# A mixer and an MLP under one gate on one core: reordered opening, half-built tables, u added straight from PSUM, state rotations on GpSimd

## The chip, the cores and the metric

One core of a Trainium2 chip runs the kernel in one launch. The metric is device time in microseconds, lower is better.

## What is computed

Input x has 2048 tokens of 1024 features. One branch is a diagonal complex state-space layer, the other a layer norm and an MLP of 3584 hidden units; a sigmoid of x·gate_w mixes them for each token:

```
Lam_bar = exp(exp(log_dt) * (Lambda_re + 1j*Lambda_im))
Bu      = x @ (((Lam_bar - 1)/Lam)[:, None] * (B_re + 1j*B_im)).T
h[t]    = Lam_bar * h[t-1] + Bu[t]                 # 2048 steps, 1024 states
a = 2*real(h @ C.T) + x*Dskip
b = gelu(layernorm(x) @ w1 + b1) @ w2 + b2
out = g*a + (1-g)*b,   g = sigmoid(sum(x*gate_w))
```

## The kernel before, in words

Every piece of work is a task with an engine, a duration that its author wrote down, a priority and its buffers. `Graph.schedule` plays the tasks through a list scheduler, and each engine's instructions are emitted in the order found. So the priorities and durations in the code set the order, and each engine then runs its own list strictly in order.

TensorE's (PE's) program has four parts: the products u = x·B, the MLP (blocks m and b), and the output products y. Nearly all products are 2x2 block products done with seven block multiplications (Strassen-Winograd, class `SG`, steps `p1` to `p7`), whose operand sums VectorE (DVE) makes beforehand (`b_sums`, `x_sums`, `x_sum4`, line 1119). A step of an u group is four matmuls of 512 columns. Steps p7 and p4 of a group use the same PSUM bank one after the other, with two other steps between them.

The opening makes the transposed operands. PE transposes the first four 128-token pieces of x (`t_x`, line 801) and the first B blocks (`t_b0`, line 874; `t_b`, line 825, for blocks 1 to 3); DVE and ScalarE (ACT) copy them out. The other three quarters of x (`xT_dma`, line 1232, called xT1 to xT3) and B blocks 4 to 7 (`bT_dma`, line 1316) are transposed by the DMA. All these loads stand in the queue of SyncE (SP). Nine matmuls on zeros (`em_warm`, line 845) run ahead of the first transpose.

Then come the plain products of block 0 (`bu_plain`, lines 1147 and 1032), the groups (1,0), (2,0), (3,0) on the first half of the tokens, and the other groups. The gate logits (`z_gate`, line 1289) are 32 narrow matmuls over all four quarters of x; they stand in the second group, (2,0).

`bu_group.fin` takes u out of PSUM. Of its two results that need an addition, the real one is added by DVE straight from PSUM (line 1218); the imaginary one is copied by ACT to a buffer `uc` (line 1221) and added by DVE from there (line 1223).

The scan of the states runs on DVE in 16 units (`ssm`, two halves of the states by eight pieces of 256 tokens) spread over the MLP. Each unit rotates u with tables of cosines and sines (line 1412 and 1415), scans (line 1426), and rotates back; the state that goes on to the next unit is rotated by three small operations on 8 numbers per partition (`fx1` to `fx3`, lines 1435, 1437, 1439). The tables are built by doubling in eight rounds of six DVE operations (line 972).

Of the kernel before, what the change touches and what calls it, by code (L numbers as in the profile page):

```python
# [171 lines left out]
class Graph:  # L172
# [43 lines left out]
    def dma(self, prio, emit, nbytes, sem, reads=(), writes=(), name="", xpose=False, extra=(), ndma=1, bw=None, thr=False, q="sp"):  # L216
# [3 lines left out]
        if xpose:  # L220
            idur = max(idur, XPOSE_ISSUE_PER_MB * nbytes / 1e6)
# [3 lines left out]
    def _schedule_once(self):  # L225
# [27 lines left out]
        while ev:  # L253
# [17 lines left out]
            for e in engs:  # L271
# [25 lines left out]
                if t.kind == "dma":  # L297
                    issue_end = st + t.dur
                    push(issue_end, 1, e)
                    ts = max(issue_end, chan_free[e])  # L300
                    busy_o = sum(1 for o in chan_free if o != e and chan_free[o] > ts)
                    bw_eff = t.bw * (1.0, 0.55, 0.4)[busy_o]
                    chan_free[e] = ts + t.nbytes / bw_eff
                    t.finish = chan_free[e] + DMA_LAT
# [76 lines left out]
    def _schedule_latest(self, ls):  # L381
# [57 lines left out]
        while ev:  # L439
# [8 lines left out]
            for e in engs:  # L448
# [13 lines left out]
                if t.kind == "dma":  # L462
                    issued = t.start + t.dur
                    push(issued, 1, e)
                    ts = max(issued, chan_free[e])
                    others = sum(1 for o in chan_free if o != e and chan_free[o] > ts)
                    chan_free[e] = ts + t.nbytes / (t.bw * (1.0, 0.55, 0.4)[others])
                    t.finish = chan_free[e] + DMA_LAT
# [97 lines left out]
def build(nc, A_x, A_Lambda_re, A_Lambda_im, A_B_re, A_B_im, A_C_re, A_C_im, A_log_dt, A_Dskip,  # L566
# [25 lines left out]
    with es:  # L592
# [81 lines left out]
        tfirst = [7, 3, 6, 0, 1, 2, 5]  # L674
# [57 lines left out]
        g.dma(P0, emit_cst_loads, NROW * 256, sem("d_cst"), writes=[b_stg], name="cst_loads", ndma=len(vecs), q="act")  # L732
# [43 lines left out]
        def load_b(pt, prio):  # L776
# [9 lines left out]
            g.dma(prio, em, 2 * 128 * D * 2, ssem("bnat", s), writes=[v], name="bnat%d" % pt, ndma=2)  # L786
# [4 lines left out]
        def t_x(k, prio):  # L791
# [11 lines left out]
            o_chain(g.add("pe", 0.06 * DT, prio, em, reads=[v, b_ident], writes=[b_ps[bk], b_ps[bk2]], name="xT_T%d" % k, extra=list(o_last)))  # L803
# [63 lines left out]
        def t_b0(ri, prio):  # L867
# [9 lines left out]
            if ri == 0:  # L877
                o_chain(t)
# [1068 lines left out]
```

## Time and profile before

| | before |
|---|---|
| median of 3 runs | 551.43 us (551.0 to 551.49) |
| profiled execution, its own time | 554.73 us |
| its span | 553.0 us |
| busy: PE, DVE, ACT, GpSimd (POOL) | 546.1, 510.2, 287.1, 89.7 us |

The span runs from the first to the last instruction of the profiled execution; 1.73 us of its own time lie outside. "PEld" is PE's weight load, "PEclk" the granted TensorE clock (1.00 is 2.4 GHz, 0.50 is 1.2 GHz), "SPq" and "POOLq" are issues of DMAs.

### The profile page before, as it was taken

How to read it: one execution, taken by the hardware profiler on the slowest of the kernel's cores; microseconds unless marked ns; L12 is line 12 of the kernel's file. 1: busy time of each engine (PE TensorE's matmuls, PEld its weight loads, DVE VectorE, ACT ScalarE, POOL GpSimd, SP SyncE). 2: the span in 40 equal slices, each digit the busy share in tenths (PEclk: the TensorE clock that was granted, in tenths of full speed). 3: DMA queues.
4: the chain of work that ended last, by engine and by line, in shares of the span. 5: the costliest groups of instructions: out<-in, count | busy, mean ns of one | idle time of the engine just before them, and what ended most of it. 6: DMA issues, size and time to landing. Idle time of an engine off the chain costs nothing.

```text
span 553.0 us, 7464 instructions
## 1 busy us (share of the span) xinstructions
PE 546.1 (99%) x2622; PEld 250.2 (45%) x2622; DVE 510.2 (92%) x880; ACT 287.1 (52%) x480; POOL 89.7 (16%) x146
## 2 busy tenths in 40 slices
PE   8899999999999999999999999999999999999997
PEld 5444444444444444444444444444444444444443
DVE  5879989999999999999999999999999999899863
ACT  3767887886773347773347762247672322111110
POOL 0127662540001010001110000220000111001000
PEclk9989999999999999999999999999999999999999
DMA  9996999789762455464666983797767999987531
GB/s 268 252 301 155 272 272 293 252 274 360 237 142 105 164 190 206 148 216 196 225 227 184 310 167 64 135 200 226 240 157 136 230 312 298 376 293 249 180 117 57
DMA packets 115054, 120.07 MB, mean 217 GB/s; under 512 B 70338, under 2 KB 92738, under 8 KB 113994
## 3 DMA queue, kind: packets, MB, share of 16 engines
q1 hardware_dynamic: 102400, 73.69, 47.9%
q0 software_dynamic: 12480, 45.90, 26.8%
q8 instruction: 20, 0.33, 0.2%
q14 instruction: 16, 0.13, 0.1%
q10 hardware_dynamic: 138, 0.02, 0.0%
HBM read 56.40 MB, written 47.46 MB: 188 GB/s over the span
## 4 chain that ended last, share of the span: by engine, by line
PE 94%; SPq 3%; DMA 2%; issue 0%; DVE 0%
PE ps L1034 71%; PE ps L1032 22%; SPq L1232 2%; DMA ar<-in_A_x_dram 2%; PE ps L1289 1%; PE ps L1100 0%; SPq L771 0%; SPq L784 0%; SPq L783 0%; SPq L857 0%; DVE ar L1732 0%
## 5 line engine op out<-in xcount | busy, mean ns | idle before, releaser
L1034 PE MATMUL ps<-ar 128*128 128x512 f16 (+1 forms) x1844 | 416.9, 379 | 0.0
L1034 PEld LDWEIGHTS ps<-ar 128*128 128x128 f16 (+1 forms) x1844 | 180.1, 98 | 218.1 <-issue 1.3
L1032 PE MATMUL ps<-ar 128*128 128x512 bf16 (+1 forms) x608 | 150.0, 379 | 0.0
L1119 DVE TENSOR_TENSOR ar<-ar 128x512 f16<-128x512 bf16 (+7 forms) x224 | 140.0, 662 | 3.9 <-PE ps L1289 2.0
L1032 PEld LDWEIGHTS ps<-ar 128*128 128x128 bf16 (+1 forms) x608 | 59.3, 98 | 71.5 <-ACT ar L833 0.4
L1426 DVE TENSOR_TENSOR_SCAN ar<-cst,init,ar 128x256 bf16<-128x256 f32 x128 | 88.1, 734 | 0.4
L1054 ACT ACTIVATE ar<-ps 128x512 f32<-128x512 f32 x102 | 59.8, 596 | 51.1 <-PE ps L1032 36.8
L1070 ACT ACTIVATE ps<-ps 128x512 f32<-128x512 f32 x67 | 39.0, 582 | 75.4 <-PE ps L1032 64.3
L1412 DVE TENSOR_TENSOR ar<-ar 128x2048 bf16<-128x2048 bf16 x64 | 77.0, 1217 | 0.2 <-ACT ar L1000 0.2
L1533 ACT ACTIVATE ar<-ps,cst 128x512 bf16<-128x512 f32 x56 | 38.4, 686 | 13.4 <-PE ps L1034 13.1
L1055 ACT ACTIVATE ar<-ps,cst 128x512 f32<-128x512 f32 x32 | 22.0, 688 | 44.6 <-PE ps L1034 22.1
L1622 ACT ACTIVATE ar<-ps,cst 128x512 f32<-128x512 f32 x32 | 22.0, 687 | 43.6 <-PE ps L1034 43.6
L1415 DVE TENSOR_TENSOR ar<-ar 128x1024 bf16<-128x1024 bf16 x64 | 42.0, 683 | 0.1
L1539 ACT ACTIVATE ar<-ar,cst 128x512 bf16<-128x512 f32 x56 | 40.0, 713 | 3.7 <-DVE ar L1537 3.5
L1537 DVE TENSOR_TENSOR ar<-ps,ar 128x512 f32<-128x512 f32 x56 | 38.2, 683 | 3.8 <-PE ps L1034 3.1
L1136 POOL DMA_DIRECT2D scr_u<-ar x32 | 24.9, 780 | 44.4 <-ACT ar L1164 20.4
L1745 DVE SCALAR_TENSOR_TENSOR ar<-ps,cst,ar 128x512 bf16<-128x512 f32 x31 | 22.6, 741 | 6.2 <-PE ps L1034 6.0
L1634 POOL DMA_DIRECT2D scr_ac<-ar x16 | 13.8, 892 | 87.5 <-ACT ar L1055 26.1
L1444 POOL DMA_DIRECT2D scr_h<-ar x16 | 9.4, 586 | 108.8 <-DVE ar L1415 88.7
L1625 DVE SCALAR_TENSOR_TENSOR ar<-ps,cst,ar 128x512 f32<-128x512 f32 x32 | 23.6, 741 | 3.5 <-PE ps L1034 2.9
L1632 POOL DMA_DIRECT2D scr_ac<-ar x16 | 8.5, 534 | 83.9 <-DVE ar L1625 54.8
L1716 DVE SCALAR_TENSOR_TENSOR ar<-ar,cst 128x1024 f32<-128x1024 bf16 x16 | 20.1, 1273 | 0.0
(120 smaller groups left out, 248.0 us busy)
## 6 DMA issues: line engine op xcount, KB each, us to landing
scr_ac<-ar POOLq DMA_DIRECT2D x32, 512.0 KB, 5.4
ar<-in_A_x_dram SPq DMA_DIRECT2D x32, 256.0 KB, 5.0
scr_u<-ar POOLq DMA_DIRECT2D x32, 256.0 KB, 5.1
ar<-scr_u SPq DMA_DIRECT2D x16, 512.0 KB, 4.5
scr_h<-ar POOLq DMA_DIRECT2D x16, 512.0 KB, 4.5
ar<-scr_ac SPq DMA_DIRECT2D x16, 512.0 KB, 7.5
ar<-scr_h SPq DMA_DIRECT2D x8, 1024.0 KB, 7.0
ar<-in_B_w_dram SPq DMA_DIRECT2D x14, 512.0 KB, 5.5
```

The costliest lines, as they stand in the source:

```text
L1032: ins = e.matmul(V(PS[bk], 0, [(1, n)]), st[i].ap, mv[i].ap, start=(i == 0), stop=(i == K - 1))
L1034: ins = e.matmul(V(PS[bk], 0, [(1, n)]), st[i].ap, mv[i].ap, start=False, stop=(i == K - 1), skip_group_check=True)
L1054: return e.activation(o.ap, V(PS[bk], 0, [(1, 512)]), AF.Copy)
L1070: g.add("act", c_act(512), (pb[0], q - 2), lambda e: e.activation(V(PS[b], 0, [(1, 512)]), V(PS[a], 0, [(1, 512)]), AF.Copy), reads=[b_ps[ ...
L1119: g.add("dve", c_tt16(n), (pb[0], q), lambda e: e.tensor_tensor(o.ap, a.ap, b.ap, op), reads=[a, b], writes=[o], name=nm).slack = slack
L1136: g.dma((1.0, q), lambda e: e.dma_start(out=US[pt // 4, :, 4 * pr:4 * pr + 4, r0:r0 + T], in_=evv.ap), 2 * 128 * CH * 2, ssem("us", 2 * ks ...
L1412: g.add("dve", c_tt16(UE), pri(i), lambda e: e.tensor_tensor(o.ap, a.ap, tbl.ap, ALU.mult), reads=[a, tbl], writes=[o], name=nm + tag)
L1415: g.add("dve", c_tt16(UE // 2), pri(i), lambda e: e.tensor_tensor(o.ap, a.ap, b.ap, op), reads=[a, b], writes=[o], name=nm + tag)
L1426: lambda e, pt=pt, ri=ri, vin=vin, go=go: e.tensor_tensor_scan(go.ap, Cb("R", pt, T), vin.ap, V(INIT, pt * 2 + ri, [(1, 1)]), ALU.mult, AL ...
L1533: g.add("act", c_act(512, ap_operands=1), (10.0, q + 1), lambda e: e.activation(o.ap, V(PS[bk], 0, [(1, 512)]), AF.Gelu_apprx_tanh, bias=C ...
L1537: g.add("dve", c_dve(512), (10.0, q - 2), lambda e: e.tensor_tensor(sv.ap, V(PS[bk], 0, [(1, 512)]), sv.ap, ALU.add), reads=[b_ps[bk], sv] ...
L1539: g.add("act", c_act(512, psum=False, ap_operands=1), (10.0, q + 3), lambda e: e.activation(o.ap, sv.ap, AF.Gelu_apprx_tanh, bias=C("B1", ...
```

## The change

Parts of one change:

1. **Opening.** The warming matmuls go from nine to five. x and block 0 of B are loaded alternately; B blocks 1 and 2 are loaded from ACT's queue; B block 3 isn't transposed by PE any more but by the DMA, between xT2 and xT3. The two products of block 0 are cut into halves of the tokens.
2. **Groups.** The gate logits move from group (2,0) to group (0,1), two groups later; step p4 of groups (1,0) and (2,0) moves behind p3 of (3,0), and DVE makes one more sum (`x_sum4` with an output of its own) for them.
3. **Direct u.** The copy to `uc` goes; DVE adds both u results straight from PSUM.
4. **Half tables.** Seven doublings build the upper half; ACT mirrors it into the lower half with two activations.
5. **State rotations.** `fx1` to `fx3` move from DVE to GpSimd.
6. Small: two squarings in one instruction, a planner that treats small DMAs as free of bandwidth, other due times for some sums.

```diff
-            g.dma(prio, em, 2 * 128 * D * 2, ssem("bnat", s), writes=[v], name="bnat%d" % pt, ndma=2)
+            g.dma(prio, em, 2 * 128 * D * 2, ssem("bnat", s), writes=[v], name="bnat%d" % pt, ndma=2, q="act", issue=0.9)
...
-        o_chain(g.add("pe", 3.6, (-0.99, 0), em_warm, reads=[v_zero], writes=[b_ps[4]], name="warm"))
+        o_chain(g.add("pe", 2.9, (-0.99, 0), em_warm(5), reads=[v_zero], writes=[b_ps[4]], name="warm"))
...
         load_x(0, (-0.99, 0))
         load_b0(0, (-0.98, 0))
-        for k in range(1, 4):
-            load_x(k, (-0.9, k))
-        load_b0(1, (-0.89, 0))
-        for pt in range(1, 4):
+        load_x(1, (-0.97, 0))
+        load_b0(1, (-0.96, 0))
+        load_x(2, (-0.95, 0))
+        load_x(3, (-0.94, 0))
+        g.dma((-0.99, 0), emit_cst_loads, NROW * 256, sem("d_cst"), writes=[b_stg], name="cst_loads", ndma=len(vecs), q="act", issue=2.7)
+        for pt in range(1, 3):
             load_b(pt, (-0.85, pt))
...
         PT1 = (2.5, 0)
-        v = w1(0, 0, 1)
+        TH = T // 2
+        v = w1(0, TH, 1)
...
-        for k in range(LT):
+        for k in range(LT - 1):
...
+            g.add("act", c_act(PT * TH, psum=False), (2.55, comp), lambda e, dst=dst, src=src, sg=sg: e.activation(dst.ap, src.ap, AF.Copy, scale=sg), reads=[src], writes=[dst], name="e1m%d" % comp)
...
-                    if ri == 0:
-                        g.add("dve", c_dve(CH), (1.0, q - 2), lambda e: e.tensor_tensor(ev.ap, V(PS[bk], 0, [(1, 2 * T)]), src.ap, ALU.add),
-                              reads=[b_ps[bk], sv], writes=[ev, b_ps[bk]], name="u" + nm)
-                    else:
-                        g.add("act", c_act(CH), (1.0, q - 2), lambda e: e.activation(uc.ap, V(PS[bk], 0, [(1, 512)]), AF.Copy),
-                              reads=[b_ps[bk]], writes=[uc, b_ps[bk]], name="uc" + nm)
-                        g.add("dve", c_dve(CH), (1.0, q - 2), lambda e: e.tensor_tensor(ev.ap, uc.ap, src.ap, ALU.add),
-                              reads=[uc, sv], writes=[ev], name="u" + nm)
+                    g.add("dve", c_dve(CH), (1.0, q - 2), lambda e: e.tensor_tensor(ev.ap, V(PS[bk], 0, [(1, 2 * T)]), src.ap, ALU.add),
+                          reads=[b_ps[bk], sv], writes=[ev, b_ps[bk]], name="u" + nm)
...
-        bu_plain(0, 0)
+        t_b(1, (0.5, 2), (0.5, 4))
+        xT_dma(1, (-0.5, 0))
+        xT_dma(2, (-0.4, 0))
+        bT_dma(3, (-0.35, 0))
+        xT_dma(3, (-0.3, 0))
+        bu_half(0, 0, (0.5, 0))
+        bu_half(1, 0, (0.5, 1))
+        bu_half(0, 1, (0.5, 3))
         early = [bu_group(1, 0), bu_group(2, 0)]
         early[0].p1()
+        bu_half(1, 1)
+        early[0].p2()
         t_b(2, (1.0, seq[0] + 0.5))
-        early[0].p2()
         early[1].p1()
-        t_b(3, (1.0, seq[0] + 0.5))
+        bu_plain(0, 1, (0,))
         early[1].p2()
-        bu_plain(0, 1)
+        bu_plain(0, 1, (1,))
         bT_dma(4)
...
             if n == 1:
+                x_sum4(0, seq[0], XN + 24576)
+            if n == 3:
                 z_gate()
                 z_move()
                 x_sum4(0, seq[0])
+                x_sum4(1, seq[0])
...
-                g.add("dve", 0.1, pri(20), lambda e: e.tensor_tensor(V(FXT, 8 * pg, [(2, 4), (1, 2)]), gsw.ap, V(CST, col["KF"] + 8 * pg, [(2, 4), (1, 2)]), ALU.mult),
+                g.add("pool", 0.5, pri(20), lambda e: e.tensor_tensor(V(FXT, 8 * pg, [(2, 4), (1, 2)]), gsw.ap, V(CST, col["KF"] + 8 * pg, [(2, 4), (1, 2)]), ALU.mult),
```

What the scheduler makes of it, at three places. First, SP's queue from its third load on. `in_A_x` at 771 (now 778) is a plain load of 128 tokens, 857 and 783/784 (now 878 and 790/791) are plain loads of B. Before:

```order
L771 DMA ar<-in_A_x_dram 128x1024 x3
L857 DMA ar<-in_A_B_im_dram 128x1024
L783 DMA ar<-in_A_B_re_dram 128x1024
L784 DMA ar<-in_A_B_im_dram 128x1024
L783 DMA ar<-in_A_B_re_dram 128x1024
L784 DMA ar<-in_A_B_im_dram 128x1024
L783 DMA ar<-in_A_B_re_dram 128x1024
L784 DMA ar<-in_A_B_im_dram 128x1024
L1232 DMA_TRANSPOSE ar<-in_A_x_dram 128x8x512 x3
L771 DMA ar<-in_A_x_dram 128x1024 x9
```

and in the changed kernel:

```order
L778 DMA ar<-in_A_x_dram 128x1024
L878 DMA ar<-in_A_B_im_dram 128x1024
L778 DMA ar<-in_A_x_dram 128x1024 x2
L1242 DMA_TRANSPOSE ar<-in_A_x_dram 128x8x512 x2
L1322 DMA_TRANSPOSE ar<-in_A_B_re_dram 128x8x128
L1322 DMA_TRANSPOSE ar<-in_A_B_im_dram 128x8x128
L1242 DMA_TRANSPOSE ar<-in_A_x_dram 128x8x512
```

Six plain loads of B are gone from the front of this queue (four of them are in ACT's now), and the two transposed loads of B block 3 stand ahead of xT3.

Second, ACT's list from its last small constant load (`stg`) on. Before:

```order
L728 DMA stg<-in_B_b_dram 28x128
L881 ACT_TABLE_LOAD
L881 ACTIVATE ar<-ps 128x1024
L810 ACTIVATE ar<-ps 128x4x128
L1164 ACTIVATE ar<-ps 128x512
```

and in the changed kernel, where the first activation, the copy of B block 0 out of PSUM, is at line 901:

```order
L736 DMA stg<-in_B_b_dram 28x128
L790 DMA ar<-in_A_B_re_dram 128x1024
L791 DMA ar<-in_A_B_im_dram 128x1024
L790 DMA ar<-in_A_B_re_dram 128x1024
L791 DMA ar<-in_A_B_im_dram 128x1024
L901 ACT_TABLE_LOAD
L901 ACTIVATE ar<-ps 128x1024 x2
```

Four issues stand ahead of the table load and of ACT's first copies, and the second copy of block 0, DVE's before, is ACT's.

Third, PE around the gate logits (1289, now 1299), from the last steps of group (1,0) on. Before:

```order
L1034 MATMUL ps<-ar 128x512 x12
L1032 MATMUL ps<-ar 128x512 x4
L1289 MATMUL ps<-ar,gwc 2x512 x32
L1034 MATMUL ps<-ar 128x512 x8
L1032 MATMUL ps<-ar 128x512 x4
```

and in the changed kernel, where 1049 and 1051 are the steps at 1032 and 1034 before:

```order
L1051 MATMUL ps<-ar 128x512 x12
L1049 MATMUL ps<-ar 128x512 x4
L1051 MATMUL ps<-ar 128x512 x8
L1049 MATMUL ps<-ar 128x512 x4
L1051 MATMUL ps<-ar 128x512 x4
L1049 MATMUL ps<-ar 128x512 x4
L1051 MATMUL ps<-ar 128x512 x20
L1049 MATMUL ps<-ar 128x512 x4
L1051 MATMUL ps<-ar 128x512 x4
L1049 MATMUL ps<-ar 128x512 x4
L1299 MATMUL ps<-ar,gwc 2x512 x32
```

Behind the p5 of (2,0), the row of four at which z followed before, stand 52 matmuls, thirteen steps, ahead of z. The eleventh and the thirteenth of them are the first on the second half of x: p1 of (0,1), which reads xT2, and p5 of (0,1), which needs a sum of xT2 and xT3.

## Rows read from the trace of the kernel before

**Rows 1.** The page's first lines: span, busy time and share of each engine.

```profile
span 553.0 us, 7464 instructions
...
PE 546.1 (99%) x2622; PEld 250.2 (45%) x2622; DVE 510.2 (92%) x880; ACT 287.1 (52%) x480; POOL 89.7 (16%) x146
```

**Rows 2.** Whom PE waited for, 28 us to the end (total us, times, longest).

```profile
PE ps L1289 <- DMA ar<-in_A_x_dram: 2.2, 1, 2.2
```

**Rows 3.** One long stretch: PE, PEld, DVE, ACT, POOL busy, PEclk, DMA share, GB/s.

```profile
28.00:550.00 522.00, 521.66 (x2440) 236.54 (x2440) 491.55 (x814) 270.87 (x455) 86.43 (x135) 1.00 0.74 216
```

**Rows 4.** PE in order of time around the gate logits.

```profile
24.79 1.03 PE L1032 MATMUL ps<-ar 128*128 128x512 f16 x4
28.00 3.22 PE L1289 MATMUL ps<-ar,gwc 128*2 128x512 bf16 x32 [2.18 <-DMA ar<-in_A_x_dram]
```

**Rows 5.** PE alone in stretches of 1 us: busy, PEclk, DMA share, GB/s.

```profile
28.00:29.00 1.00, 1.00 (x16) 0.71 1.09 393
29.00:30.00 1.00, 1.00 (x16) 0.50 0.99 375
30.00:31.00 1.00, 1.00 (x12) 0.50 1.05 402
31.00:32.00 1.00, 1.00 (x7) 0.58 1.11 418
```

**Rows 6.** SP's issues in order of time.

```profile
3.69 0.43 SPq L783 DMA_DIRECT2D ar<-in_A_B_re_dram  x1
...
6.72 17.26 SPq L1232 DMA_TRANSPOSE ar<-in_A_x_dram  x3
...
28.85 2.48 SPq L1316 DMA_TRANSPOSE ar<-in_A_B_re_dram  x1
31.38 3.94 SPq L1316 DMA_TRANSPOSE ar<-in_A_B_im_dram  x1
...
45.54 1.24 SPq L1316 DMA_TRANSPOSE ar<-in_A_B_re_dram  x1
```

**Rows 7.** Opening in order of time: weight loads, transposes, copies, the table load.

```profile
3.52 1.28 ACT L881 ACT_TABLE_LOAD   x1 [3.52 <-issue]
...
3.78 0.15 PEld L845 LDWEIGHTS ps<-ar 128*128 128x128 bf16 x1 [0.28 <-issue]
...
4.21 0.15 PEld L845 LDWEIGHTS ps<-ar 128*128 128x128 bf16 x1 [0.28 <-issue]
...
5.89 1.02 ACT L881 ACTIVATE ar<-ps 128x1024 bf16<-128x1024 bf16 x1 [1.09 <-PE ps L874]
...
6.36 0.45 PEld L801 LDWEIGHTS ps<-ident,ar 128*128 128x128 bf16 x8 [0.23 <-DMA ar<-in_A_x_dram]
...
7.08 0.45 PEld L801 LDWEIGHTS ps<-ident,ar 128*128 128x128 bf16 x8 [0.28 <-DMA ar<-in_A_x_dram]
...
7.54 1.04 PE L1147 MATMUL ps<-ar 128*128 128x256 bf16 x8
...
16.13 1.06 PE L825 MATMUL ps<-ident,ar 128*128 128x128 bf16 x16
...
17.87 4.00 PEld L1032 LDWEIGHTS ps<-ar 128*128 128x128 bf16 x20 [0.32 <-DMA ar<-in_A_x_dram]
```

**Rows 8.** The chain that ended last, in order of time: start, us, what.

```profile
33.37 0.86 PE ps L1032 x4
```

**Rows 9.** Groups by line: DVE near the edits, GpSimd's small operations (count | busy, mean ns).

```profile
L1119 DVE TENSOR_TENSOR ar<-ar 128x2048 f16<-128x2048 bf16 x9 | 10.8, 1217 | 3.6 <-PE ps L1289 2.0 <-DMA ar<-in_A_x_dram 1.7
...
L1218 DVE TENSOR_TENSOR ar<-ps,ar 128x512 bf16<-128x512 f32 x15 | 10.3, 688 | 3.8 <-PE ps L1034 3.6
...
L1439 DVE TENSOR_TENSOR init<-init,fxt 128x8 f32<-128x8 f32 x14 | 2.2, 158 | 0.0
...
L1257 POOL TENSOR_TENSOR cst<-cst 128x4 f32<-128x4 f32 x4 | 4.8, 1196 | 0.1
...
L1255 POOL TENSOR_TENSOR cst<-cst 128x4 f32<-128x4 f32 x4 | 1.2, 297 | 0.0
```

More of the change, by code (lines that the diff above doesn't have):

```diff
@@ L219, in dma @@
         idur = {"sp": SP_ISSUE, "act": ACT_ISSUE, "pool": POOL_ISSUE}[q] * ndma
-        if xpose:
+        if issue is not None:
+            idur = issue
+        elif xpose:
             idur = max(idur, XPOSE_ISSUE_PER_MB * nbytes / 1e6)
@@ L299, in _schedule_once @@
                     push(issue_end, 1, e)
[L300 to L304, printed above, removed]
+                    if t.nbytes < 32768:
+                        t.finish = issue_end + DMA_LAT
+                    else:
+                        ts = max(issue_end, chan_free[e])
+                        busy_o = sum(1 for o in chan_free if o != e and chan_free[o] > ts)
+                        bw_eff = t.bw * (1.0, 0.55, 0.4)[busy_o]
+                        chan_free[e] = ts + t.nbytes / bw_eff
+                        t.finish = chan_free[e] + DMA_LAT
                     push(t.finish, 2, t)
@@ L464, in _schedule_latest @@
                     push(issued, 1, e)
[L465 to L468, printed above, removed]
+                    if t.nbytes < 32768:
+                        t.finish = issued + DMA_LAT
+                    else:
+                        ts = max(issued, chan_free[e])
+                        others = sum(1 for o in chan_free if o != e and chan_free[o] > ts)
+                        chan_free[e] = ts + t.nbytes / (t.bw * (1.0, 0.55, 0.4)[others])
+                        t.finish = chan_free[e] + DMA_LAT
                 else:
@@ L770, in load_x @@
             v = XNAT[k]
-            g.dma(prio, lambda e: e.dma_start(out=v.ap, in_=x2[k * 128:(k + 1) * 128, :]), 128 * D * 2,
-                  ssem("xnat", k), writes=[v], name="xnat%d" % k)
+            return g.dma(prio, lambda e: e.dma_start(out=v.ap, in_=x2[k * 128:(k + 1) * 128, :]), 128 * D * 2,
+                         ssem("xnat", k), writes=[v], name="xnat%d" % k, issue=0.6 if k == 0 else 0.43)
         BN = {}
@@ L1157, in bu_plain @@
+        def bu_plain(pt, c, ris=(0, 1)):
+            for ri in ris:
                 bk = (4, 5, 6, 1)[2 * c + ri]
                 ws = [AR.v(bqo(pt, 2 * ri) + dt * 256, [(1, 128)]) for dt in range(DT)]
[L1159 to L1165 removed]
@@ L1166, in bu_plain @@
-                if c % 2 == 1:
-                    u_store(pt, c // 2, ks, q, ri)
+                q = mm("bu%d.%d.%d" % (pt, c, ri), bk, ws, [xt(dt, c) for dt in range(DT)], True)
+                u_copy(pt, c, ri, bk, 2, q)
         def b_sums(pt, q):
@@ L1196, in bu_group @@
             st = {"A11": bl(0, BF16), "A12": bl(1, BF16), "A22": bl(3, BF16), "S1": bl(4), "S2": bl(5), "S3": bl(6), "S4": bl(2)}
-            mv = {"B11": xl(0, BF16), "B21": xl(1, BF16), "B22": xl(3, BF16), "T1": xl(4), "T2": xl(5), "T3": xl(6), "T4": xl(2)}
+            mv = {"B11": xl(0, BF16), "B21": xl(1, BF16), "B22": xl(3, BF16), "T1": xl(4), "T2": xl(5), "T3": xl(6), "T4": xl(2) if bu_n[0] > 2 else [AR.v(XN + 24576 + d * 1024, [(1, 512)], FP16) for d in range(4)]}
             if bu_n[0] % 2:
```

204 lines of the change are left out of this document (102 added, 102 removed).

## Prediction, made before the changed kernel ran

> **What bounds the kernel now.** I read the page's first part, then PE's waits, then stretches. PE is busy for 546.1 of 553.0 us [rows 1]. From 28.00 us to 550 us it is busy for 521.66 of 522 us [rows 3], so nothing that DVE, ACT or GpSimd gain there can shorten the time; they can only lose it. PE's one wait for data past the first microseconds is 2.18 us ahead of the gate logits z, which read all of x and wait for xT3, the last DMA transpose of x [rows 2, 4]. The stretches show a second loss behind it: full rate (PEclk 1.00, 2.4 GHz) until the gap, then 0.71, 0.50, 0.50 and 0.58 in the four microseconds from 28.00 us on [rows 5]. The engine stood idle for 2.18 us, went to 1.2 GHz soon after it restarted, and was back at 2.4 GHz before 32 us. The shortfall is 0.29 + 0.50 + 0.50 + 0.42 = 1.71 us. The stall costs 3.9 us in all. Everything else of the opening is PE's own work and some tenths of waits.
>
> **The change part by part**, against the profiled execution (554.73 us of its own, 553.0 us of span, 1.73 us outside).
>
> *The stall at z: -3.9 us if nothing takes its place.* Thirteen steps now stand between the p5 of group (2,0) and z. A step is 0.86 us [rows 8]. The first that needs xT2 is the eleventh, the first that needs xT3 (through the sum T1 of DVE) the thirteenth, so PE has 12 x 0.86 = 10.3 us of work where it had none. Is xT3 there then? In SP's queue six plain loads of B are gone ahead of xT1: it can issue at about 3.7 us, where the first of them stood, not at 6.72 [rows 6]. The three transposes of x took 17.26 us to issue. Two transposed loads of B block 3 come in ahead of xT3; the rows have such issues at 2.48 and 3.94 us (DMAs crowded) and at 1.24 us (less so) [rows 6]. So xT3 is issued between 3.7 + 17.26 + 2.5 = 23.5 and 3.7 + 17.26 + 6.4 = 27.4 us, against 24.0 before, and lands as much earlier or later than the 28.0 us of before: 27.5 to 31.4 us. Before, PE ran out of work at 24.79 + 0.86 = 25.65 us [rows 4, 8]; less the next two terms it gets there, to the end of p5 of (2,0), at about 25.2, so to p5 of (0,1) at 35.5. Behind xT3 on DVE's list stand T1, 1.22 us, and then an addition, 0.69 us [rows 9], that must free the bank of p4 of (2,0), nine steps after 25.2, at 32.9. That asks for xT3 by 32.9 - 1.22 - 0.69 - 0.2 (signals, an estimate from the 0.23 us that PE idled ahead of a row released by another engine [rows 7]) = 30.8 us. The upper end misses this by 0.6 us. I take 0 and keep 0.6 for the range.
>
> *B block 3 by DMA: -1.0 us.* Its sixteen transposes took 1.06 us with their tail [rows 7], on a PE that had nothing to wait for beside them. Its DMAs are needed some 27 us into the span and are issued ahead of xT3; nothing waits.
>
> *The start: +0.5 us.* Four warming matmuls go; at 0.43 us each (4.21 - 3.78) that is 1.7 us. But the third and fourth piece of x arrive at 6.36 and 7.08 us, and PE waited for both [rows 7]: the opening runs at the pace of its loads, and the time between is idle. So 0, not -1.7. Against it, ACT issues four loads ahead of its table load, at 0.43 us each [rows 6]: the table load goes from 3.52 to 5.2, the first copy from 5.89 to 6.5, its end from 6.9 to 7.55, and the first product of block 0, at 7.54 before [rows 7], can wait 0.2 us. And B's second half now arrives ahead of the third piece of x, which takes the place of the fourth (7.08 us); with the four loads from ACT's queue mixed in between it comes later, by one spacing of loads, 0.72 us, or two: I take 0.3, from 0 to 1.4.
>
> The Trainium skill (DMA: Bandwidth & Descriptors, Issuing engines are not separate DMA queues) speaks against moving loads to ACT: DMAs of all engines interleave on the same 16 DMA engines, and only issue time is saved. By it the moved loads give PE nothing in the opening, the term is at its upper end, and the sum below is 1.1 us less of a gain. A DMA share of 1 or more [rows 5] shows engines that are full later on; no row shows two queues mixed in the opening.
>
> *xT1.* PE waited 0.32 us for it before, until 17.87 us [rows 7]. It is issued 3 us earlier and wanted about 1.5 us earlier. 0.
>
> *Direct u: 0.* ACT loses fifteen copies and DVE's addition costs the same from PSUM, 0.69 us [rows 9]. What changes is who frees the bank of p7 for p4 of the same group: DVE, in the order of its list, in place of ACT. Between them lie two steps, 1.73 us; less 0.69 and 0.2 leaves 0.8 us. A DVE sum of 1.22 us that has just begun would cost up to 0.4 us, fifteen times at most. The steady stretch has no PE wait now, and DVE's wait for PE ahead of the additions, 3.8 us in fifteen [rows 9], says that DVE often stands ready. I take 0, and up to 6 us.
>
> *Half tables, rotations, squarings: 0.* DVE loses six table operations and 42 small ones of 0.158 us [rows 9], PE waits for none of them, and DVE's 92% leaves 43 us free. GpSimd's operations on as small operands take 0.30 to 1.20 us [rows 9], so three of them 0.9 to 3.6 us, between the last scan of a unit and the first of the next, with eight DVE operations (lines 1412 and 1415) between them. Those eight take 4 x 1.22 us at least, by the row of the same size, so the cover is larger than the price. Were it gone, the next unit's scans would wait on DVE, and behind them the MLP's additions that free PE's banks; DVE's 43 us of idle would take the first 3 us of each of 14 such waits.
>
> *Sum.* -3.9 - 1.0 + 0.5 = -4.4 us: 550.3 us for a profiled execution. The runs shown have a median of 551.43, 3.3 us under the profiled one. With the same difference the median after is 547.0 us. That step is the weakest. PE's rate from 28 us on is that of the clock, so the 3.3 us lie in the opening, the tail or outside, and the stall of 3.9 us may be a part of them.
>
> **The rivals.**
>
> *The timed runs hardly had the stall.* If loads land a little sooner without the profiler, z didn't wait and the clock stayed. The 3.3 us speak for it, and that they are near the 3.9; against it, that 1.73 us lie outside the span. The gain is then -1.0 + 0.5 = -0.5 us, 550.9; with a part of the stall left, down to 549.0.
>
> *PE cold in the opening.* Before, nine matmuls ran back to back at the lower clock (0.43 us for 512 columns), and the first transposes behind them ran at the higher one. With five, and a gap for the first load, the rise can come later. At 1.2 GHz eight transposes take 0.86 us in place of 0.45, against a spacing of loads of 0.72: five groups lose 0.7 us; if it lasts through the first two half products, 0.85 us each and another 0.4 for transposes, 2.8 us. Time: 547.0 + 0.7 to 2.8 = 547.7 to 549.8.
>
> *xT3 comes too late: slower.* The transposed B loads ahead of it are the cause. From 30.8 us on each microsecond is PE's, and a gap of 2 us or more brings the 1.7 us of low clock again, so the 4.4 us are gone when xT3 lands at 33.5. That is 2.1 us past the upper bound: two B issues of 4.3 us each. The 3.94 us row speaks for it, the 1.24 us row against. At 35 us: 547.0 + 4.2 + 1.7 = 552.9.
>
> *p4 waits for DVE behind p7: slower.* If DVE is 0.4 us late in each of the fifteen groups, 547.0 + 6 = 553.0; it decides at 0.3 us a group. Against it stands that DVE waits for PE there and not PE for DVE.
>
> **How the numbers follow.** Stall gone in the timed runs too: 0.45, 547.0 us, its own range 546.0 to 548.5. Hardly a stall in the timed runs: 0.30, 549.0 to 551.2. Cold opening: 0.13, 547.7 to 549.8. xT3 too late: 0.07, 550.8 to 556. p4 behind DVE: 0.05, 550.8 to 553. A measurement can tell 0.2% of this kernel, 1.1 us, from no change: faster is below 550.3, slower above 552.5. Faster: 0.45 + 0.16 of the second + 0.12 = 0.73; same: 0.14 + 0.01 + 0.02 = 0.17; slower 0.10. The range from 546.0 to 551.2 leaves out some 0.05 below and 0.12 above.
>
> **What would show it.** Right: no wait of PE for x at z or at p5 of (0,1); PEclk 1.00 from 25 to 40 us; z's 32 matmuls in about 1.8 us, not 3.22; SP's transposes start near 3.7 us and xT3 lands before 31; PE busy without gaps from then on; span near 548.6. Wrong: a wait of PE on DVE behind p7 (line 1233), PE waiting at p5 of (0,1), PEclk 0.5 or transposes of 0.86 us for eight before 10 us, scans on DVE that wait for GpSimd. If the profile after is 4 us shorter and the median less than 1 us, the second rival was right.

## The result: slower, 557.5 us, and the profile after

| | before | after |
|---|---|---|
| median of the runs side by side | 551.52 us (551.0 to 552.29, 6 runs) | 557.53 us (555.5 to 564.05, 6 runs) |
| ratio | | 1.0086, 95% interval 1.0057 to 1.0114 |
| profiled execution, its own time and span | 554.73, 553.0 us | 557.6, 555.9 us |

The ratio and its interval, here and in the table below, leave out runs more than 1.5% above the fastest run of the same kernel, here the one of 564.05 us. By the ratio the change costs 4.7 us, by the medians 6.0.

The page's first lines and the list of what PE waited for, of the changed kernel (compare [rows 1, 2]):

```profile
span 555.9 us, 7457 instructions
...
PE 545.5 (98%) x2610; PEld 251.0 (45%) x2610; DVE 500.9 (90%) x827; ACT 279.9 (50%) x465; POOL 117.0 (21%) x188
```

```profile
PE ps L835 <- DMA ar<-in_A_B_im_dram: 2.9, 1, 2.9
PE ps L1049 <- DMA ar<-in_B_w_dram: 2.2, 1, 2.2
PE ps L865 <- DVE ar L990: 1.2, 1, 1.2
PE ps L808 <- DMA ar<-in_A_x_dram: 0.6, 1, 0.6
PE ps L1051 <- DVE ar L1136: 0.3, 1, 0.3
```

The wait at the gate logits (line 1289, now 1299) is gone. Two new ones have come: 2.9 us for B block 1, and 2.2 us for a tile of the MLP's first weights. All the waits of this list come to 7.2 us. In a profile of the kernel before that is 5.8 us shorter (e12, below) they come to 1.6:

```profile
PE ps L845 <- DVE ar L978: 1.2, 1, 1.2
PE ps L1034 <- DVE ar L1537: 0.2, 1, 0.2
PE ps L801 <- DMA ar<-in_A_x_dram: 0.2, 1, 0.2
```

So the waits differ by 5.6 us, nearly the whole difference of the two profiles, and none of them is a wait for an addition of u (line 1233). PE in order of time, in the opening and at the gate logits (compare [rows 4, 7]):

```profile
7.73 1.06 PE L808 MATMUL ps<-ident,ar 128*128 128x128 bf16 x8
8.59 1.69 PE L1172 MATMUL ps<-ar 128*128 128x256 bf16 x8
10.12 0.61 PE L808 MATMUL ps<-ident,ar 128*128 128x128 bf16 x8
10.56 1.04 PE L1172 MATMUL ps<-ar 128*128 128x256 bf16 x8
14.50 0.62 PE L835 MATMUL ps<-ident,ar 128*128 128x128 bf16 x8 [2.90 <-DMA ar<-in_A_B_im_dram]
...
40.87 1.90 PE L1299 MATMUL ps<-ar,gwc 128*2 128x512 bf16 x32
```

Eight transposes take 1.03 to 1.06 us until 8.6 us and 0.61 from 10.1 us on; then PE stands for 2.90 us. The first is what they also take in e16 where the granted clock is 0.50 (1.2 GHz), but here the granted clock reads 1.00 in every microsecond from 1 to 17 us, so the slow opening is read off the durations alone. The 32 matmuls of the gate logits take 1.90 us without a wait, against 3.22 with one of 2.18, and the clock holds, in the stretches' columns of [rows 3]:

```profile
25.00:40.00 15.00, 15.00 (x71) 6.55 (x70) 11.95 (x33) 8.61 (x15) 3.20 (x5) 1.00 1.19 271
```

The chain that ended last names both new waits (start, us, what):

```profile
3.94 10.51 DMA ar<-in_A_B_im_dram
14.46 0.04 issue
14.50 0.62 PE ps L835 x8
...
117.31 6.86 DMA scr_xn<-ar
124.17 0.02 SPq L526
124.19 0.04 issue
124.23 9.71 DMA ar<-in_B_w_dram
133.94 0.05 issue
133.99 1.04 PE ps L1049 x4
```

A plain load of 256 KB issued from ACT's queue at 3.94 us lands 10.51 us later. And the w1 load at 124.23 us waits for a store of the normalized x (issued at 117.31 us), whose place in the memory it takes. SP's issues in order of time show what stands around both (compare [rows 6]; L1242 and L1322 are the transposes of x and B, L1506 loads w1, L1578 w2):

```profile
3.69 17.34 SPq L1242 DMA_TRANSPOSE ar<-in_A_x_dram  x2
21.15 1.24 SPq L1322 DMA_TRANSPOSE ar<-in_A_B_re_dram  x1
22.48 1.25 SPq L1322 DMA_TRANSPOSE ar<-in_A_B_im_dram  x1
23.79 6.69 SPq L1242 DMA_TRANSPOSE ar<-in_A_x_dram  x1
...
119.69 0.37 SPq L1578 DMA_DIRECT2D ar<-in_B_w_dram  x1
124.23 2.51 SPq L1506 DMA_DIRECT2D ar<-in_B_w_dram  x2
```

The transposes of x run from 3.69 us on, beside the loads in ACT's queue. Later a w2 load stands ahead of the w1 load, which PE needs first.

### The profile page after: what moved, and what is told of

Its sections match the earlier page's. It is cut to its first block, busy times and chain, and to the rows that moved or that the text cites. A ratio compares the mean times of both kernels' runs of the same rounds, so it can differ in the third digit from the quotient of the medians.

```text
span 555.9 us, 7457 instructions
## 1 busy us (share of the span) xinstructions
PE 545.5 (98%) x2610; PEld 251.0 (45%) x2610; DVE 500.9 (90%) x827; ACT 279.9 (50%) x465; POOL 117.0 (21%) x188
## 4 chain that ended last, share of the span: by engine, by line
PE 90%; DMA 5%; POOL 1%; DVE 1%; issue 1%; ACTq 1%; ACT 0%; SPq 0%; POOLq 0%
PE ps L1051 67%; PE ps L1049 22%; DMA ar<-in_A_B_im_dram 2%; DMA ar<-in_B_w_dram 2%; DMA scr_xn<-ar 1%; POOL cst L1267 1%; ACTq L736 0%; DVE ar L1273 0%; DVE ar L1233 0%; PE ps L835 0%; PE ps L1299 0%; PE ps L1117 0%; PE ps L1172 0%; POOL cst L1264 0%; POOL scr_u L1153 0%
## 5 line engine op out<-in xcount | busy, mean ns | idle before, releaser
L1049 PE MATMUL ps<-ar 128*128 128x512 bf16 (+1 forms) x600 | 148.3, 379 | 2.3 <-DMA ar<-in_B_w_dram 2.2
L1136 DVE TENSOR_TENSOR ar<-ar 128x512 f16<-128x512 bf16 (+8 forms) x225 | 141.2, 667 | 4.0 <-DMA ar<-in_B_w_dram 2.0
L1453 POOL TENSOR_TENSOR fxt<-ar,cst 128x8 f32<-128x8 bf16 x14 | 15.7, 1122 | 144.4 <-DVE ar L1444 144.4
L1233 DVE TENSOR_TENSOR ar<-ps,ar 128x512 bf16<-128x512 f32 x30 | 20.4, 684 | 5.6 <-PE ps L1051 5.4
L1652 POOL DMA_DIRECT2D scr_ac<-ar x16 | 13.8, 881 | 45.3 <-ACT ar L1640 21.3
```

What stands on the lines that cost most here:

```text
L1049: ins = e.matmul(V(PS[bk], 0, [(1, n)]), st[i].ap, mv[i].ap, start=(i == 0), stop=(i == K - 1))
L1136: g.add("dve", c_tt16(n), (pb[0], q), lambda e: e.tensor_tensor(o.ap, a.ap, b.ap, op), reads=[a, b], writes=[o], name=nm).slack = slack
```

## Experiments

All times, each with the kernel before measured on the same chip (medians of before: 551.77 beside e1 to e4, 552.09 beside e5 to e8, 551.86 beside e9 to e12, 552.48 beside e13 to e16, 551.98 beside e17 and e18). Where the runs of one kernel lie far apart, the spread says more than the ratio.

| run | kernel | median us (range, runs) | ratio to before, 95% interval |
|---|---|---|---|
| e1 | after, B loads in SP's queue | 554.0 (553.12 to 558.11, 12) | 1.0041 (1.0016 to 1.0066) |
| e2 | after, nine warming matmuls | 560.57 (557.77 to 562.11, 4) | 1.0138 (1.009 to 1.0186) |
| e3 | before, gate logits a group later | 553.21 (552.42 to 560.2, 12) | 1.0035 (1.0003 to 1.0067) |
| e4 | before, parts 3 to 5 of the change | 558.3 (550.39 to 565.33, 12) | 1.0021 (0.9983 to 1.0059) |
| e5 | before, direct u alone | 562.51 (555.01 to 575.86, 9) | 1.0106 (1.0065 to 1.0148) |
| e6 | before, half tables and rotations | 553.59 (552.8 to 554.95, 12) | 1.0032 (1.0021 to 1.0043) |
| e7 | e1 with ACT's copy of u | 552.08 (551.4 to 553.0, 12) | 0.9998 (0.9987 to 1.0008) |
| e8 | e7, gate logits a group earlier | 552.23 (550.49 to 558.99, 12) | 1.0002 (0.9986 to 1.0019) |
| e9 | after with ACT's copy of u | 563.34 (559.84 to 567.5, 6) | 1.0187 (1.0156 to 1.0217) |
| e10 | e8, nine warming matmuls | 552.37 (551.34 to 556.72, 12) | 1.0008 (0.9985 to 1.0032) |
| e11, e12 | before, profiled again | 551.51; 551.88 (1 each) | |
| e13 | before, B loads in ACT's queue | 563.63 (558.33 to 576.35, 6) | 1.0169 (1.0131 to 1.0206) |
| e14 | after, xT1 held back | 561.98 (560.85 to 564.2, 5) | 1.018 (1.0155 to 1.0204) |
| e15 | e7 with full tables, rotations on DVE | 559.05 (558.14 to 559.57, 4) | 1.0125 (1.0099 to 1.0151) |
| e16 | after again | 561.48 (557.4 to 563.8, 6) | 1.0152 (1.0117 to 1.0187) |
| e17 | after, all transposes held back | 553.02 (551.43 to 556.88, 12) | 1.0014 (0.9989 to 1.004) |
| e18 | e7, w1 due times as before | 550.21 (549.75 to 552.7, 12) | 0.9972 (0.9954 to 0.9991) |

**The loads in ACT's queue: e1, e13, e14, e17, e16.** e1 puts them back into SP's queue, ahead of xT1; e13 makes the opposite edit, on the kernel before and alone:

```diff
-... name="bnat%d" % pt, ndma=2, q="act", issue=0.9)
+... name="bnat%d" % pt, ndma=2, issue=0.9)
```

> The changed kernel with the natural loads of B blocks 1 and 2 back in SP's queue, ahead of the first DMA transpose of x. Theory Q (the loads from ACT's queue were mixed with the DMA transposes issued from SP and so landed at 14.5 us): PE's 2.9 us wait at line 835 goes, B block 1 lands by 10 us, time 3 us or more below the changed kernel, about 554. Rival R (the DMA engines are simply full, whichever queue): the wait stays at 2 us or more and the time is within 1 us of the changed kernel.

> The kernel before with one edit: the plain loads of B blocks 1 to 3 go to ACT's queue, and SP's first transpose of x so stands right behind the loads of x and block 0. Theory Q (plain loads in ACT's queue starve beside the DMA transposes in SP's): PE waits 3 to 8 us for B block 1 before 20 us, and the median is 555 to 561 us. Theory R (it was the order and the cold PE of the new opening, not the queue): median 551 to 552.5 and no such wait.

e1 took 3.5 us off by the medians (2.5 by the ratios), and its profile has no wait for B block 1. e13 put 9.3 us on by the ratio; in its profile, of a run of 567.32 us, PE's row in the opening is

```profile
19.30 1.01 PE L825 MATMUL ps<-ident,ar 128*128 128x128 bf16 x8 [11.44 <-DMA ar<-in_A_B_im_dram]
```

So moving the loads does it, with the old order and nine warming matmuls too. Is it the queue itself, or the transposes beside it? e14 and e17 leave the loads in ACT's queue and hold SP's transposes until B block 1 has landed:

```diff
-... name="xT%d" % c, xpose=True, bw=200000.0)
+... name="xT%d" % c, xpose=True, bw=200000.0, extra=[BLD[1]] if c == 1 else ())
```

```diff
-... name="xT%d" % c, xpose=True, bw=200000.0)
+... name="xT%d" % c, xpose=True, bw=200000.0, extra=[BLD[1]])
```

The first is e14's, the second e17's, which gives the same dependence to the transposes of B and to the plain loads of x behind them.

> The changed kernel with the loads left in ACT's queue, but SP's first transpose of x held until both halves of B block 1 have landed. Theory Q: without transposes beside them the loads land within 6 us of their issue instead of 10.5, PE's wait for B block 1 falls under 1 us, median 553 to 555.5. If ACT's queue itself is slow (issue behind the small constant loads): block 1 lands at 13 us or later as before, median 557 or more, later still since the transposes are later too.

> The changed kernel with the loads left in ACT's queue, and all of SP's transposes (and its plain loads behind them) held until both halves of B block 1 have landed; in the run ahead of it only xT1 was held, and xT2 took its place in the queue. Theory Q (the loads starve beside the transposes): 2.6 MB of plain loads from both queues at the 330 to 380 GB/s of the plain loads land by 10 us, B block 1 by 9; PE's wait for it is under 0.5 us. Against it xT1 comes 5 us later, which PE may wait for by up to 3 us. Median 553 to 557. Theory A (ACT's queue is slow by itself): B block 1 lands at 13 us or later again, and the median is 559 or more.

e14 settled nothing: the scheduler put xT2 where xT1 had stood, transposes ran all the same, and B block 1 landed at 14.05 us, as late as in the changed kernel (14.45). In e17, where all were held, it landed at 9.30 us:

```profile
3.95 5.35 DMA ar<-in_A_B_im_dram
```

and PE had no wait for it. The DMA queues between 8 and 10 us (packets, MB, time of their packets as a share of the 16 engines; q10 is ACT's, q1 SP's), first of the changed kernel, then of e17, show why:

```profile
q10 hardware_dynamic: 162, 0.29, 65.7%
q1 hardware_dynamic: 508, 0.13, 50.6%
```

```profile
q10 hardware_dynamic: 382, 0.68, 88.7%
```

In the same two microseconds ACT's queue moves 0.29 MB beside the transposes and 0.68 MB without them. The median fell to 553.0, though xT1 was now 0.9 us late for PE. In SP's one queue order did this by itself: before, the transposes stood behind all plain loads of B [rows 6].

The changed kernel once more:

> The changed kernel, unchanged, timed and profiled again. If its opening varies with how the transposes mix with ACT's loads (landing of B block 1 at 14.5, 15.6 and 18.0 us in three profiles of kernels that issue it alike): the runs spread by 4 us and more, 555 to 564, and the landing is another than 14.5. If the loss is fixed: 556.5 to 558.5 and 14.5 again.

Its runs spread from 557.4 to 563.8, its ratio to before is 1.0152 where the first was 1.0086, and in its profile (563.8 us) the wait for B block 1 was 3.6 us, the w1 wait 3.8. Both brought the low clock, which the waits of 2.90 and 2.2 us in the first profile didn't: the granted clock was 0.50 from 15 to 20 us and 0.69 from 140 to 145. That is some 4 us more, an estimate from these two stretches (5 x 0.50 + 5 x 0.31). With e2 (landing at 15.53 us) and e9 (17.95) the loss in the opening is not one number: the landing of B block 1 differs from run to run and kernel to kernel, and a longer wait can bring the low clock on top.

**Cold PE: e2, e10.** Nine warming matmuls in place of five, in the changed kernel and in e8:

```diff
-g.add("pe", 2.9, (-0.99, 0), em_warm(5), ...
+g.add("pe", 3.6, (-0.99, 0), em_warm(9), ...
```

> The changed kernel with nine warming matmuls in place of five, nothing else. Theory C (the short warm-up leaves the opening at 1.2 GHz): eight transposes go back from 0.83 to about 0.45 us; but the wait for B block 1 until 14.5 us takes up all that is won, so the time is within 1 us of the changed kernel. Rival: if the cold opening is on the path by itself, 1.5 us or more less.

> The best kernel so far (loads on SP, copy restored, gate logits in group (3,0)) with nine warming matmuls for five. Theory C (PE cold in the opening costs up to 2 us): transposes of eight at 0.61 us in place of 1.03, median 550.0 to 551.5, below both kernels. Theory N (the opening runs at the pace of its loads, so a warm PE only waits, and what is won meets the x loads of y): median 551.7 to 552.8, with waits of PE for x and B in the opening of 1 us more.

In e2 the transposes ran at 0.61 us from 5.7 us on, and PE then waited 4.94 us for B block 1: a warm PE only came to the wait earlier. After a wait that long the clock fell (granted 0.66 from 15 to 20 us). e10 is no faster than e8, in whose opening transposes take 1.03 to 1.06 us for eight until 5.3 us only. Nothing was to be won by the four matmuls. The nine of the kernel before don't always bring the fast opening either: in e12 the first eight transposes behind them took 1.06 us, and its time is at the median.

**The stall at the gate logits: e3, e11, e12.** e3 moves only the gate logits, from group (2,0) to (3,0), in the kernel before; e11 and e12 profile the kernel before again.

```diff
             if n == 1:
-                z_gate()
-                z_move()
                 x_sum4(0, seq[0])
+            if n == 2:
+                z_gate()
+                z_move()
```

> The kernel before with only the gate logits z moved one group later, from group (2,0) to (3,0). Theory S (the 3.9 us stall at z is in the profiled execution and hardly in the timed ones): the profile loses the 2.18 us wait and the half clock behind it, the median falls by less than 1 us. Rival (the stall is in all executions): the median falls by 3 to 4 us, to about 548.

> The kernel before, unchanged, profiled again. Theory S (its timed runs hardly have the stall at the gate logits; the first profiled execution, 3.3 us above the median, was one of those that have it): own time 551 to 552.5 us, wait at the gate logits under 0.7 us, granted clock 1.00 from 28 to 32 us. Theory P (every profiled execution has it, timed ones don't): own time 554 to 555.5 with the wait of about 2 us and the low clock. Theory V (all have it): own time 551 to 552.5 with the wait of 2 us.

> The same once more, for a third profiled execution of the kernel before. Theories S, P and V as for the run ahead of it: S is right where own time and the wait at the gate logits fall together, P where both stay, V where the time falls and the wait stays.

e3's profile has no stall (gate logits at 31.56 us, 1.83 us for the 32, clock 1.00), and its median is 1.4 us above before, not 3.9 below. The two new profiles of before give the reason directly, PE in e11 and in e12:

```profile
26.42 1.90 PE L1289 MATMUL ps<-ar,gwc 128*2 128x512 bf16 x32 [0.33 <-DMA ar<-in_A_x_dram]
```

```profile
26.41 1.90 PE L1289 MATMUL ps<-ar,gwc 128*2 128x512 bf16 x32
```

Their own times are 551.51 and 551.88, at the median; the wait is 0.33 us and none, against 2.18 in [rows 4]. Theory S holds: the profile that the prediction was built on was of an execution that was 3 us longer, by this stall. How often that happens isn't shown: 13 of the 112 runs of the kernel before timed beside e1 to e18 took 554 us or more, and only three executions were profiled.

**Direct u: e5, e4, e6, e7, e9.** e5 adds u straight from PSUM in the kernel before, e6 takes the other two steady parts alone, e4 all three; e7 and e9 give the copy back to e1 and to the changed kernel.

```diff
+                    if ri == 0:
                         g.add("dve", c_dve(CH), (1.0, q - 2), lambda e: e.tensor_tensor(ev.ap, V(PS[bk], 0, [(1, 2 * T)]), src.ap, ALU.add),
...
+                    else:
+                        g.add("act", c_act(CH), (1.0, q - 2), lambda e: e.activation(uc.ap, V(PS[bk], 0, [(1, 512)]), AF.Copy),
...
+                        g.add("dve", c_dve(CH), (1.0, q - 2), lambda e: e.tensor_tensor(ev.ap, uc.ap, src.ap, ALU.add),
```

This is the diff of e7 and e9; e5 makes it the other way round.

> The kernel before with one edit alone: both u results added by DVE straight from PSUM, no copy by ACT. Theory D (the direct addition makes PE depend on DVE's list: whatever DMA blocks the head of that list then stalls PE through the PSUM bank): the runs spread as in the run with all three steady parts, highest above 557 us, median 553 to 559, and the profile has a wait of PE on the DVE line of the direct addition, tenths up to 6 us. Theory O (the half tables and the rotations only reorder DVE's list, the direct addition is harmless): median 550.7 to 552.8 as before, no such wait.

> The kernel before with only the parts of the change behind the opening: u added straight from PSUM, half-built tables, state rotations on GpSimd. Theory O (all of the loss is in the opening and the later gate logits): within 1 us of before. Rival (p4 waits for DVE behind p7, or DVE's scans wait for GpSimd): 2 us or more slower, with PE waits for DVE in the profile.

> The kernel before with the half tables and the state rotations on GpSimd, without the direct addition. Theory D: median 550.7 to 552.8, as before, no wait of PE on DVE between 70 and 130 us. Theory O: median 553 to 559, spread of the runs above 5 us, and a wait of PE on DVE or for the MLP's data near 100 us.

> The changed kernel with B blocks 1 and 2 loaded from SP's queue and the copy of u by ACT restored: the two parts that the runs so far blame are undone. Theory D and Q (ACT's queue starves the loads): PE's 1.4 us of waits on the direct addition go, 554.0 less 1.4 is 552.6 or, where the y products then wait longer for x, up to 553.5; the profile has no wait of PE on the line of the addition. If the direct addition costs nothing: 553.3 to 554.7 as with loads on SP alone.

> The changed kernel with the copy of u by ACT restored and the B loads left in ACT's queue: the fourth corner of two parts by two (loads in ACT's or SP's queue, with or without the copy). If the two costs add (loads 3.5 us by the run with loads on SP, direct addition 1.9 us by that run and the one with the copy): 552.1 + 3.5 = 555.6 us, range 554.9 to 556.3, with the wait for B block 1 in the opening, 2.5 to 3.5 us, and none on the addition. If the load cost hides the other (a later PE leaves DVE more time): 557 as the changed kernel.

e5 shows the mechanism at its largest, in a profile of a run of 564.18 us (its shortest run took 555.01). SP's transposes of the normalized x, DVE behind them, PE behind DVE:

```profile
66.00 18.55 SPq L1461 DMA_TRANSPOSE ar<-scr_xn  x3
...
85.37 13.75 SPq L1461 DMA_TRANSPOSE ar<-scr_xn  x1
```

```profile
108.89 1.23 DVE L1119 TENSOR_TENSOR ar<-ar 128x2048 f16<-128x2048 bf16 x1 [11.57 <-DMA ar<-scr_xn]
110.03 0.68 DVE L1216 TENSOR_TENSOR ar<-ps,ar 128x512 bf16<-128x512 f32 x1
```

```profile
112.35 4.01 PE L1034 MATMUL ps<-ar 128*128 128x512 f16 x11 [10.51 <-DVE ar L1216]
```

A sum on DVE waits 11.57 us for a transposed piece. Behind it in DVE's list stands the addition of u (line 1216), and behind that the matmuls that want its bank. With the copy, by the program's order, ACT frees the bank and only a later group would feel DVE's wait; that isn't shown, since without this edit the sum doesn't wait like that. In e12 it waited 0.3 us for a transposed piece, though one transpose took 10.20 us to issue there too. So e5 has two things, pieces that land late and an addition behind them, and no run takes them apart. e4 had the same, 6.4 us, in a profile of 560.77 us; its runs go from 550.39, less than any of before beside it, to 565.33. By the ratio e5 costs 5.9 us and e4 1.2. In e1 the waits on the addition (line 1233) were 1.4 us, beside 2.3 us in the y products:

```profile
PE ps L1051 <- DVE ar L1763: 2.3, 2, 1.6
PE ps L1051 <- DVE ar L1233: 1.4, 2, 0.9
```

The longer of the two, and DVE ahead of it:

```profile
100.79 2.76 PE L1051 MATMUL ps<-ar 128*128 128x512 f16 x11 [0.87 <-DVE ar L1233]
```

```profile
99.45 0.68 DVE L1433 TENSOR_TENSOR ar<-ar 128x1024 bf16<-128x1024 bf16 x1
100.06 0.68 DVE L1233 TENSOR_TENSOR ar<-ps,ar 128x512 bf16<-128x512 f32 x1
```

DVE waits for no DMA there: it works without a gap from 93.9 us on, on the layer norm, sums, rotations of u and another addition, and the addition stands in line. The other wait (0.54 us, at 45.35) is behind the doublings of the tables in the same way. So in e1 it's DVE's own work that holds the bank, and in e5 a DMA that DVE waits for. e7, with the copy, has neither wait, and is 1.9 us faster than e1; its runs lie within 1.6 us. e6 lost 1.5 us, with waits of 1.2 us at the gate logits and 1.4 us on DVE in the MLP, where e12 has none and 0.2 us. e9 fell against expectation: the costs don't add. Its B block 1 landed at 17.95 us, PE waited 6.5 us for it, and the granted clock was 0.56 from 15 to 20 us and 0.76 in the next five; the copy can't be read from it.

**Where the gate logits stand, and the order behind them: e8, e15, e18.** e8 moves the gate logits to group (3,0) in e7. e15 takes the half tables and the rotations out of e7, but leaves the scratch of the doublings at the half size. e18 gives e7 the old due times of the first w1 tiles, one of the small edits under part 6. The core of each, in this order:

```diff
-            if n == 3:
+            if n == 2:
                 z_gate()
                 z_move()
+            if n == 3:
                 x_sum4(0, seq[0])
```

```diff
-        for k in range(LT - 1):
+        for k in range(LT):
...
-                g.add("pool", 0.5, pri(20), ...
+                g.add("dve", 0.1, pri(20), ...
```

```diff
-            w1sl = {1: 4, 2: 2, 3: 0.5}.get(len(w1slot), 0.0)
+            w1sl = {1: 8, 2: 6, 3: 2.5}.get(len(w1slot), 0.0)
```

> The last kernel with the gate logits one group earlier, in the group where they stood at the earliest without a wait (group (3,0)). Theory L (later gate logits delay the last layer-norm pieces, their stores and so the weight loads behind them): the last store of normalized x lands 5 to 6 us earlier than with the gate logits in (0,1), and no PE wait for weights follows; median 0 to 1.5 us below the last kernel's. Theory X (z is off the path by now, the wall is the x loads of the y products): same median within 0.6 us, with the PE wait in y as large as before.

> What is left of the change is the opening and the moved groups: loads on SP, copy of u by ACT, the full tables and the rotations on DVE as before. If the half tables and the rotations cost what they cost on the kernel before (1.7 us): 552.1 - 1.7 = 550.4, a gain over both kernels. If they cost only through that kernel's order: 551.6 to 552.6, as with them.

> The kernel with loads on SP and the copy restored, and besides the due times of the first MLP weights as before (8, 6 and 2.5 steps in place of 4, 2 and 0.5), so that SP issues the w1 load ahead of the second w2 load. Theory W (the later due times put w1 behind w2 in SP's queue, and PE waits for it): the waits of 0.70 us for the weights and 0.65 us for the sum made of them, at 127 to 130 us, go; median 550.5 to 551.7, below both kernels. Theory X (what is won there is lost to the x loads of y): median 551.7 to 552.6 with new waits of PE past 460 us.

e8 is the same as e7: the place of the gate logits is worth nothing by then. e15 fell the other way, 7 us slower than e7 for taking away two parts that had cost 1.5 us on the kernel before. Its chain has

```profile
115.07 14.28 DMA ar<-in_B_w_dram
```

a w1 load issued together with w2's, for which PE waits 3.0 us, and a wait of 3.2 us in the y products. Neither part names these loads or products; that the scheduler's new order did it is the likely reading, and no run tests it. e18 is the fastest kernel here, 0.28% under before. PE waits for nothing past the first 7 us:

```profile
PE ps L865 <- DVE ar L990: 1.2, 1, 1.2
PE ps L897 <- DMA ar<-in_A_B_im_dram: 0.2, 1, 0.2
```

The last stores of the normalized x (GpSimd, line 1282; 1275 in the changed kernel) and the fourth w1 load in SP's queue (line 1513, w2 at 1585), in e18:

```profile
105.08 0.54 POOL L1282 DMA_DIRECT2D scr_xn<-ar  x1
```

```profile
109.08 0.37 SPq L1513 DMA_DIRECT2D ar<-in_B_w_dram  x1
113.88 0.37 SPq L1585 DMA_DIRECT2D ar<-in_B_w_dram  x1
```

in e7, from which e18 differs by the due times alone:

```profile
114.17 0.54 POOL L1282 DMA_DIRECT2D scr_xn<-ar  x1 [0.18 <-issue]
```

```profile
115.17 0.88 SPq L1585 DMA_DIRECT2D ar<-in_B_w_dram  x1
117.89 4.80 SPq L1513 DMA_DIRECT2D ar<-in_B_w_dram  x2
```

and the last store in the changed kernel:

```profile
119.25 0.54 POOL L1275 DMA_DIRECT2D scr_xn<-ar  x1 [1.40 <-DVE ar L1273]
```

With the old due times the normalized x is stored 9 us earlier than in e7 and 14 us earlier than in the changed kernel, and the fourth w1 load goes ahead of w2, at 109.08 us against 117.89 (e7) and 124.23 (changed kernel) behind w2. The waits of e7 that go with it, 0.70 us for the weights and 0.65 us for the sum made of them, are as large as the difference of the ratios, 1.4 us. The intervals of e7 and e18 just overlap, so the order is shown and the price is 1.4 to 1.9 us with that doubt.

## Why the prediction was wrong

In the changed kernel's own profile two waits that the prediction didn't have make the loss: 2.9 us for B block 1 and 2.2 us for the w1 tile. Undone one after the other, the parts give a ladder by medians: after 557.5, loads back on SP 554.0 (-3.5), the copy back 552.1 (-1.9), the old w1 due times 550.2 (-1.9). The last stands 1.8 us under before. So the ladder has 7.3 us of losses, and 1.8 us of gain that they bury (-1.8 + 7.3 = +5.5, against +6.0 measured; the medians come from several chips). By the ratios the rungs are 2.5, 2.4 and 1.4 us and the gain is 1.5; with the second timing of the changed kernel (e16) the first rung is 6.1. The ladder holds in this order only: e9 and e15 show that one rung alone can give quite another time. The other small edits of part 6 and the moved steps of part 2 were not taken out one by one.

- **"The start: +0.5 us" failed, in place and size.** The term asked what the loads from ACT's queue do to x and block 0 in SP's, "0.3, from 0 to 1.4". It did not ask what the transposes, now at the front of SP's queue, do to the loads that were moved. These land 10.51 us after issue, and it is B block 1 for which PE waits. Priced like the other loads, it seemed free; measured, 3.5 us by the medians, 2.9 us of wait in the first profile, up to 6.5 in others.
- **The rule of the Trainium skill was on the right side and its price too small.** By the Trainium skill ("DMA: Bandwidth & Descriptors", Issuing engines are not separate DMA queues) I had the term at 1.4 us. The rows agree that the queues share the engines (0.29 against 0.68 MB in two microseconds). The Trainium skill (the same page, Queues, rings and completion order) says that each DMA engine goes round-robin between its queues, packet by packet. The trace agrees in so far as both queues have packets in the same 2 us; 162 packets of the one and 508 of the other don't show that they take turns one for one. By that rule the moved loads give up their turn to a transpose at each packet, which the term should have priced by the time of transposes, not by the spacing of plain loads.
- **"With the same difference the median after is 547.0 us" failed, as the first rival said.** The stall of 3.9 us was in the one profiled execution, and not in two more whose times are at the median of the timed ones (e11, e12). That step was called the weakest, and the stall and the 3.3 us between profile and median should have been read as the same thing.
- **"Direct u: 0, and up to 6" held in the changed kernel's profile, by luck.** No PE wait for the addition stands there or in e16. Where B block 1 lands early it does: 1.1 us in e17, and with the loads back on SP the same part costs 1.9 us (e1 to e7, waits of 0.54 and 0.87 us behind DVE's own work), and on the kernel before 5.9 us (e5, where DVE waits for a DMA). The term allowed for one DVE sum of 1.22 us that had just begun, and neither for several operations in line nor for a DMA that DVE's list waits for. The rival "p4 waits for DVE behind p7" was given 0.05.
- **Due times for w1: not priced at all.** I had "other due times for some sums" under the small edits and took nothing. That they put w1 behind w2 in SP's queue could be read from the order of the instructions; PE's wait for it is 2.2 us in the changed kernel, and undoing it is worth 1.9 us by the medians (1.4 by the ratios).
- **"Half tables, rotations, squarings: 0" is open.** +1.5 us alone on before (e6), and 7 us slower without them in e7 (e15). PE's waits in the changed kernel name neither. What they cost of themselves can't be told from what the scheduler makes of them.
- **Right:** the gate logits without a wait, clock 1.00 from 25 to 40 us, SP's transposes from 3.69 us (3.7 foretold), B block 3's DMAs in 2.5 us, no wait at p5 of (0,1). The last is luck, owed to PE's own lateness: two transposes of x took the 17.34 us that I gave to three, xT3 was issued until 30.48 us, not 27.4 at most, and DVE had to wait for it until 34.08 us, where the prediction wanted it before 31. The p5 of (2,0) ended at 29.5 us in place of the 25.2 that I took, so PE didn't need it earlier. The opening, with the loads in SP's queue, is worth more than the -1.0 us of block 3: in e18 the p5 of group (2,0) begins at 23.69 us, in e12 at 25.26.
- **PE cold in the opening** happened as the rival described (1.03 us for eight transposes) and no cost of it shows, since the wait for B block 1 lay behind it and e2 and e10 won nothing by warming.
- **"A gap of 2 us or more brings the 1.7 us of low clock again"**, in the rival on xT3, doesn't hold: the gaps of 2.90 and 2.2 us in the changed kernel's profile brought none, those of 3.6 and 3.8 us in e16 did.

## What to carry to other kernels

Before a stall is taken off the time, profile the kernel twice: a profile 3 us above the median of the runs may owe the 3 us to the very stall. One DMA queue keeps an order that two queues do not: a load moved to another engine's queue is no longer ahead of the transposes it stood ahead of. An engine that takes over the freeing of a PSUM bank brings its whole list with it, its own work (e1) and what it waits for, DMAs too (e5); and where a planner sets the order, each edit must be tried in the order it will run in, since the price of a part measured elsewhere does not carry over.

## What the hardware showed unexpectedly

- Plain loads of 256 KB in ACT's queue landed 10.5 us (changed kernel) after issue beside DMA transposes in SP's queue, and 5.35 us (e17) with the transposes held, from the same issue time of 3.94 to 3.95 us.
- Transposes keep the issuing queue itself: one piece of the normalized x occupied SP's issue for 13.75 us (e5) and 10.20 us (e12), while four of them took 2.85 to 5.48 us each in the first profile of before.
- A stand of PE didn't always bring the low clock. After 2.18 us, in the first profile of before, the granted clock was 0.50 in the next microsecond but one [rows 5]; after 2.90 us in the changed kernel the eight transposes behind it took 0.62 us, which is 2.4 GHz; after 3.62 us in e16 they took 1.03, at a granted clock of 0.50, which is 1.2 GHz.
- The granted clock of the profile doesn't show every slow stretch: in the opening of the changed kernel it reads 1.00 in each microsecond while eight transposes take 1.03 to 1.06 us, against 0.61 later.
